# Batch 0's stored rows split by group, its gather and its constants in a new order on the DMA queue

## The chip, the cores and the metric

One core of a Trainium2 chip runs the kernel. The metric is the device time of one execution in microseconds (us), the median of several. Its engines each have a queue that is worked in order: TensorE (PE: matmuls, with the weight loads PEld beside them), VectorE (DVE), ScalarE (ACT), GpSimd (POOL) and SyncE (SP), which computes nothing here and issues every DMA.

## The reference

Eight batches of 3136 rows by 256 columns go through two stages. The first is a spectral layer: a real Fourier transform along the rows, a complex 256x256 mix with bias, a soft threshold, and the transform back. The second is a feed-forward layer with a three-tap convolution in its gate.

```python
X = np.fft.rfft(x, axis=1)
Yr = Xr @ w_r - Xi @ w_i + b_r
Yi = Xr @ w_i + Xi @ w_r + b_i
Y  = sign(Y) * max(|Y| - 0.01, 0)           # real and imaginary part alike
y  = np.fft.irfft(Yr + 1j * Yi, n=3136, axis=1)
h  = max(y @ w_in, 0)
out = (h * sigmoid(conv3(h, conv_w))) @ w_out
```

## The kernel before

The transform of 3136 = 56 x 56 points is taken in two steps by matmuls with tables. All work of the spectral layer is cut in units of four: four of 28 row pairs (JC) in stage 1, four of 28 frequency units (UG) in stage 2, mix and stage 3. So each batch has NG = 7 pieces of either kind, and there are 56 items (batch, group).

- **Stage 1** (`stage1`, and `stage1_head` for batch 0): one piece of x, a tile `xr` of 112 partitions by 4 x 256, is multiplied with the table `f1` in two matmuls; the two results are copied to an SBUF tile (`a1`, in the head `ha0` to `ha6`) and stored in DRAM as `sc1[b]` (112 rows, 28, 256). A piece fills all 112 rows, but only four of the 28 columns.
- **Stage 2** (`load_a2`, `stage2`): group g of a batch needs 16 of the 112 rows of `sc1[b]`, namely rows 16g to 16g + 15, with all 28 columns, so parts of all seven pieces. `load_a2` gathers them in a tile `a2` in one DMA. 16 matmuls with the table `t2` (one slice per group, `load_t2(g)`) follow; ACT and DVE split the result in a high and a low part (`fh`, `fl`, with `d` for the difference of the two components).
- **Mix** (`mix`): 36 matmuls with the mix weights `wmix_hi` and `wmix_lo`; then DVE adds `bias` (`p1`) and makes the sums `v`, ACT and DVE the threshold, ACT and POOL the split for stage 3.
- **Stage 3** (`stage3`): 12 matmuls with the table `i1_hi`, `i1_lo`, one copy, and a store to `sc2[b]`. It runs three items behind stage 2. The table comes in seven pieces (`load_inv1`), each loaded to a staging tile with the tag `raw` (two buffers, which the raw mix weights `wm_raw` use too) and split by an ACT cast and a DVE subtraction.

The main loop runs over the items: load `a2` for item it + 2, stage 2 of it, in the first seven turns a piece of the inverse table and the next slice of `t2`, mix of it - 1, stage 3 of it - 3, and up to a few pieces of stage 1 of later batches (`p1` counts them). From item 3 on, some background work converts the feed-forward weights. The feed-forward layer follows the loop.

Ahead of the loop stands the start, which the change is about: `load_f1`; the seven x pieces of batch 0 (the first in two halves); then, all queued behind the last x load, `load_t2(0)`, `load_mix` (the loads of both mix weights, and their conversion: `wmix_hi` by ACT casts at L140, `wmix_lo` at L141 and `wm` at L157 by DVE), `load_bias` (four loads), and `stage1_head`, in which ACT evicts the first and DVE the second matmul of each piece and SP stores the piece whole (L267). Behind the last of these stores are queued two pieces of stage 1 of batch 1 and `load_a2` of items 0 and 1; behind the second of these, everything else.

The order within each engine's queue is made by a planner, once for the whole program, from the order in which the code is traced, the dependencies, and its own estimate of times. `tc.issue_after(ins)` adds an edge by hand: what is traced in its block goes behind `ins` in the queue of `ins`'s engine. A DMA that SP issues has one of eight completion counters; the counters are used in turn, so the n-th DMA is issued only when the one eight before it has landed. A DMA that reads what another wrote waits in SP's queue until that one has landed.

Of the kernel before, what the change touches and what calls it, by code (L numbers as in the profile page):

```python
# [24 lines left out]
UG = 4  # L25
NG = U // UG
JC = 4
# [68 lines left out]
def spectral_ffn_kernel(ctx: ExitStack, tc: tile.TileContext, x, w_r, w_i, b_r, b_i,  # L96
                        w_in, conv_w, w_out, fwd1, fwd2, inv1, inv2, out):
    nc = tc.nc
    K1, K2 = 2 * R, 2 * SP

    dram = ctx.enter_context(tc.tile_pool(name="dram", bufs=1, space=DRAM))
    sc1 = [dram.tile([K1, H, D], F32, name=f"sc1_{b}") for b in range(B)]
# [15 lines left out]
    with ExitStack() as ab:  # L118
# [20 lines left out]
        def split(dst_hi, dst_lo, src):  # L139
            nc.scalar.copy(dst_hi, src)  # L140
            nc.vector.tensor_tensor(dst_lo, src, dst_hi.bitcast(F32), op=ALU.subtract)  # L141
# [4 lines left out]
        def load_t2(g):  # L146
            nc.sync.dma_start(t2[:, g * UG:(g + 1) * UG, :], fwd2v[:, g * UG:(g + 1) * UG, :])

        def load_mix():

            raw = [stg.tile([P, NT, D], F32, name=f"wm_raw{k}", tag="raw", bufs=2) for k in range(2)]
            for k in range(2):
                nc.sync.dma_start(raw[k], (w_r, w_i)[k].rearrange("(t p) e -> p t e", p=P))
            split(wmix_hi[:, :, 0, :], wmix_lo[:, :, 0, :], raw[1])
            for k, op in ((1, ALU.subtract), (2, ALU.add)):
                w = stg.tile([P, NT, D], F32, name="wm", tag="wm")
                nc.vector.tensor_tensor(w, raw[0], raw[1], op=op)  # L157
                split(wmix_hi[:, :, k, :], wmix_lo[:, :, k, :], w)

        def load_bias():  # L160
            for c in range(2):
                for k in range(UG // 2):
                    nc.sync.dma_start(bias[:, c, k, :], (b_r, b_i)[c].partition_broadcast(P))
# [77 lines left out]
        def stage1(b, jc):  # L241

            xr, _ = load_x(s1p, b, jc, bufs=XRB)
            a1 = s1p.tile([K1, JC, D], F32, name="a1", bufs=2)
            for j in range(0, JC, 2):
                ps = ps1.tile([K1, 2, D], F32, name="ps_s1")
                nc.tensor.matmul(ps, f1, xr[:, j:j + 2, :], start=True, stop=True)  # L247
                nc.scalar.copy(a1[:, j:j + 2, :], ps)
            return nc.sync.dma_start(sc1[b][:, jc * JC:(jc + 1) * JC, :], a1)

        def stage1_head(xs, b=0):

            with tc.tile_pool(name="ha", bufs=1, reuse_waits="tile") as ha:
                for jc, xr in enumerate(xs):
                    a1 = ha.tile([K1, JC, D], F32, name=f"ha{jc}")
                    for j in range(0, JC, 2):
                        k = (jc * 2 + j // 2) % 4
                        if k < 3:
                            ps = psm.tile([K1, 2, D], F32, name="ps_s1h", tag=f"ps_mx{k}")
                        else:  # L260
                            ps = ps1.tile([K1, 2, D], F32, name="ps_s1")
                        nc.tensor.matmul(ps, f1, xr[:, j:j + 2, :], start=True, stop=True)
                        if j:
                            nc.vector.tensor_copy(a1[:, j:j + 2, :], ps)
                        else:
                            nc.scalar.copy(a1[:, j:j + 2, :], ps)
                    st = nc.sync.dma_start(sc1[b][:, jc * JC:(jc + 1) * JC, :], a1)  # L267
            return st

        def load_a2(b, g):  # L270
            a2 = a2p.tile([K1, UG, D], F32, name="a2")
            ld = nc.sync.dma_start(a2, sc1[b].rearrange("(u q) j d -> (q j) u d", q=4)[:, g * UG:(g + 1) * UG, :])
            return a2, ld
# [65 lines left out]
        nc.vector.memset(warm, 0.0)  # L339
        nc.scalar.activation(warm, warm, AF.Sigmoid)  # L340

        AHEAD = NG + 3
        items = [(b, g) for b in range(B) for g in range(NG)]
        n_it = len(items)
        WP0, LAST = 3, n_it - 6
        a2s = {}
        p1 = NG
        load_f1()
        with tc.tile_pool(name="hx", bufs=1, reuse_waits="tile") as hx:
            xh = []  # L350
            for p in range(NG):
                xr, ld = load_x(hx, 0, p, parts=2 if p == 0 else 1, tag=f"hx{p}")
                xh.append(xr)
            with tc.issue_after(ld.ins):
                load_t2(0)
                load_mix()
                load_bias()
                st = stage1_head(xh)
        with tc.issue_after(st.ins):
            for _ in range(2):  # L360
                stage1(*items[p1])
                p1 += 1
            for i in range(2):
                a2s[i], ld = load_a2(*items[i])
        ab.enter_context(tc.issue_after(ld.ins))
        wkf, wk, cab, io = [ab.enter_context(tc.tile_pool(name=nm, bufs=n, reuse_waits="tile"))
                            for nm, n in (("wkf", 2), ("wk", 2), ("cab", 1), ("io", 2))]
        i1_hi = cab.tile([K2, U, K1], F32R, name="i1_hi")
# [124 lines left out]
    for st in range(n_st + LAG):  # L493
        if st < n_st:
# [8 lines left out]
            if todo and f in (1, 4, 7):  # L503
                b, jg = todo.pop(0)
# [28 lines left out]
```

## Time and profile before

| | us |
|---|---|
| median of 3 runs | 1789.02 (1785.93 to 1789.36) |
| the profiled execution | 1792.41 |
| its span, first to last instruction | 1790.6 |
| TensorE busy in it | 1750.6 |
| VectorE busy in it | 1539.0 |
| ScalarE busy in it | 1225.7 |

The rows further down come from the one profiled execution; their times count from the first instruction of its span. In a row of the timeline stand the start, the duration, engine, line and operation, the tile written and those read, and in brackets the idle time before it and what ended that. An fp32 matmul leaves two records, so a piece of stage 1 has four. In the table of stretches "(x38)" is the number of records in the stretch, PEclk the granted share of TensorE's full clock (2.4 GHz; the lower level is 1.2), and the DMA share is that of 16 DMA engines.

### The profile page before, as it was taken

What the parts mean: (1) busy time and instruction counts of PE and PEld (TensorE: products, weight loads), DVE (VectorE), ACT (ScalarE), POOL (GpSimd) and SP (SyncE); (2) the same over time, 40 slices, a digit from 0 to 9 for tenths busy, and PEclk for the clock granted to TensorE, in tenths of its full rate; (3) what the DMA queues carried; (4) which work ended last, traced back from release to release, by engine and by line L of the source; (5) the groups of instructions that cost most, each with busy time, mean ns of one, the idle gap of its engine ahead of it and who ended that gap; (6) DMA issues with size and microseconds to landing.
All of it is one profiled execution on the core that took longest, in us unless ns stands there. A gap on an engine that the chain in (4) does not pass through costs nothing.

```text
span 1790.6 us, 29395 instructions
## 1 busy us (share of the span) xinstructions
PE 1750.6 (98%) x12096; PEld 1640.0 (92%) x12096; DVE 1539.0 (86%) x1840; ACT 1225.7 (68%) x1581; POOL 133.5 (7%) x60
## 2 busy tenths in 40 slices
PE   5989999999998999999999999999999999999998
PEld 2878889889988999999999999999999999999998
DVE  2989999999997888888888888888888888888887
ACT  2657766666665677777777677777767767777766
POOL 0112222222222000000000000000000000000000
PEclk8999999999999999999999999999999999999999
DMA  9766676676535111111011011111101111100001
GB/s 267 234 218 210 186 231 213 189 236 203 159 99 152 40 52 32 32 52 52 32 53 52 21 33 51 53 50 51 50 27 42 52 42 42 42 22 21 21 22 42
DMA packets 107382, 164.63 MB, mean 92 GB/s; under 512 B 8816, under 2 KB 86000, under 8 KB 107248
## 3 DMA queue, kind: packets, MB, share of 16 engines
q1 hardware_dynamic: 107248, 162.74, 29.8%
q8 instruction: 96, 1.57, 0.4%
q14 instruction: 38, 0.31, 0.1%
HBM read 85.65 MB, written 77.07 MB: 91 GB/s over the span
## 4 chain that ended last, share of the span: by engine, by line
PE 88%; DVE 6%; DMA 2%; issue 1%; ACT 1%; SPq 0%; ACTq 0%; DVEq 0%
PE acc L468 31%; PE ps_h L440 31%; PE ps_mx L306 10%; PE ps_s L421 5%; PE ps_s L282 4%; PE ps_s L247 4%; PE ps_s L333 3%; DVE v L315 2%; DMA i_raw<-in_inv_dram 1%; DVE fl L290 1%; DVE fl L288 1%; DVE p L311 1%; DVE v L321 1%; DMA sc<-ha 0%; DVE d L287 0%
## 5 line engine op out<-in xcount | busy, mean ns | idle before, releaser
L468 PE MATMUL acc<-wout,gh 128*128 128x256 f32 x3136 | 577.2, 283 | 0.0
L449 DVE SCALAR_TENSOR_TENSOR c<-h,cst_s,c 128x896 f32<-128x896 f32 x448 | 512.7, 1146 | 53.2 <-ACT c L447 52.2
L440 PE MATMUL ps_h<-yh,win 128*128 128x450 f32 x1792 | 552.0, 368 | 1.4 <-ACT yh L427 1.2
L468 PEld LDWEIGHTS acc<-wout,gh 128*128 128x128 f32 x3136 | 501.0, 191 | 6.8
L468 PE MATMUL acc<-wout,gl 128*128 128x256 f32 x1568 | 441.9, 283 | 0.0
L442 ACT ACTIVATE h<-ps_h 128x900 f32<-128x900 f32 x224 | 207.5, 926 | 266.9 <-PE ps_h L440 266.7
L440 PEld LDWEIGHTS ps_h<-yh,win 128*128 128x128 f32 x1792 | 340.1, 190 | 27.1 <-ACT yh L427 1.4
L440 PE MATMUL ps_h<-yl,win 128*128 128x450 f32 x896 | 329.7, 368 | 0.7 <-DVE yl L428 0.7
L468 PEld LDWEIGHTS acc<-wout,gl 128*128 128x128 f32 x1568 | 298.7, 191 | 0.2
L455 DVE TENSOR_TENSOR gl<-c,gh 128x896 fp32r<-128x896 f32 x224 | 242.8, 1088 | 56.4 <-ACT gh L454 52.5
L451 DVE TENSOR_TENSOR c<-h,c 128x896 f32<-128x896 f32 x224 | 243.2, 1086 | 48.9 <-ACT c L450 48.6
L454 ACT CAST gh<-c 128x896 fp32r<-128x896 f32 x224 | 209.8, 943 | 49.3 <-DVE c L451 49.3
L450 ACT ACTIVATE c<-c 128x896 f32<-128x896 f32 x224 | 213.3, 952 | 26.0 <-DVE c L449 23.0
L306 PE MATMUL ps_mx<-wmix_lo,fh 128*128 128x256 f32 x672 | 204.1, 304 | 0.0
L306 PE MATMUL ps_mx<-wmix_hi,fh 128*128 128x256 f32 x672 | 200.3, 298 | 1.0 <-DVE cw_e L188 0.7
L306 PE MATMUL ps_mx<-wmix_hi,fl 128*128 128x256 f32 x672 | 191.8, 287 | 6.4 <-DVE fl L290 6.2
L440 PEld LDWEIGHTS ps_h<-yl,win 128*128 128x128 f32 x896 | 169.9, 190 | 11.6 <-DVE yl L428 1.0
L447 ACT ACTIVATE c<-h,cst_s 128x896 f32<-128x896 f32 x168 | 175.5, 1044 | 2.5
L323 POOL TENSOR_TENSOR sl<-v,sh 128x1024 fp32r<-128x1024 f32 x56 | 133.3, 2380 | 437.2 <-PE ps_s L333 277.2
L315 DVE TENSOR_TENSOR v<-ps_mx,p 64x512 f32<-64x512 f32 x224 | 153.9, 687 | 3.3
L306 PEld LDWEIGHTS ps_mx<-wmix_hi,fl 128*128 128x128 f32 x672 | 128.0, 191 | 18.3 <-issue 9.7
L306 PEld LDWEIGHTS ps_mx<-wmix_lo,fh 128*128 128x128 f32 x672 | 128.8, 192 | 12.3 <-issue 12.3
(86 smaller groups left out, 2037.6 us busy)
## 6 DMA issues: line engine op xcount, KB each, us to landing
a<-sc SPq DMA_DIRECT2D x56, 448.0 KB, 4.8
sc<-z SPq DMA_DIRECT2D x56, 448.0 KB, 3.2
z<-sc SPq DMA_DIRECT2D x56, 448.0 KB, 3.7
xr<-in_x_dram SPq DMA_DIRECT2D x55, 448.0 KB, 4.9
out_dram<-o SPq DMA_DIRECT2D x27, 896.0 KB, 4.2
sc<-a SPq DMA_DIRECT2D x49, 448.0 KB, 5.1
sc<-ha SPq DMA_DIRECT2D x7, 448.0 KB, 5.8
win_bits<-in_moe_w_in_dram SPq DMA_DIRECT2D x4, 512.0 KB, 7.4
```

The lines of the kernel that those rows point to most:

```text
L306: nc.tensor.matmul(ps[c][:, k, :], lt, rh, start=(n == 0), stop=(n == len(mm) - 1))
L315: nc.vector.tensor_tensor(v[dst, :, k, :], ps[c][src], p1[src, c], op=ALU.add)
L323: SL_ENG.tensor_tensor(sl, v, sh.bitcast(F32), op=ALU.subtract)
L440: nc.tensor.matmul(ps[:, a, 0:CH + 2], lt, rh, start=(n == 0), stop=(n == len(mm) - 1))
L442: nc.scalar.activation(h, ps[:, :, 0:CH + 2], AF.Relu)
L447: nc.scalar.mul(c, h[:, :, 0:CH], cw[:, 0, f:f + 1])
L449: nc.vector.scalar_tensor_tensor(c, h[:, :, k:k + CH], cw[:, k, f:f + 1], c, op0=ALU.mult, op1=ALU.add)
L450: nc.scalar.activation(c, c, AF.Sigmoid)
L451: nc.vector.tensor_tensor(c, h[:, :, 1:CH + 1], c, op=ALU.mult)
L454: nc.scalar.copy(gh, c)
L455: nc.vector.tensor_tensor(gl, c, gh.bitcast(F32), op=ALU.subtract)
L468: nc.tensor.matmul(acc[m // 2][:, m % 2, :], lt[:, sl], rh[:, f, :], start=(f == 0 and n == 0 and m % 2 == 0), stop=(f == NF - 1 and n == ...
```

## The change

- The seven stores of batch 0 become fourteen: of each piece, the 16 rows that group 0 needs (`rows` 0 to 15) are stored apart from the other 96.
- These stores stand in an order written out by hand, each queued behind the one before: the 16 rows of pieces 0 to 4, the other rows of piece 0, the 16 rows of piece 5, the other rows of piece 1, the 16 rows of piece 6, then the gather `load_a2` of item 0, then the other rows of pieces 2 to 6.
- Behind the last store stands the gather of item 1, behind it the four bias loads, the two pieces of stage 1 of batch 1 (with their x loads), and all the rest.
- The two raw mix weights are loaded ahead of the first slice of `t2`, and converted (`make_mix`) behind the last two evictions of the head on ACT and DVE.

No byte more or less is moved, and no matmul, copy or addition is added or removed.

```diff
--- before.py
+++ after.py
@@ -147,10 +147,13 @@
             nc.sync.dma_start(t2[:, g * UG:(g + 1) * UG, :], fwd2v[:, g * UG:(g + 1) * UG, :])
 
         def load_mix():
-
             raw = [stg.tile([P, NT, D], F32, name=f"wm_raw{k}", tag="raw", bufs=2) for k in range(2)]
             for k in range(2):
                 nc.sync.dma_start(raw[k], (w_r, w_i)[k].rearrange("(t p) e -> p t e", p=P))
+            return raw
+
+        def make_mix(raw):
+
             split(wmix_hi[:, :, 0, :], wmix_lo[:, :, 0, :], raw[1])
             for k, op in ((1, ALU.subtract), (2, ALU.add)):
                 w = stg.tile([P, NT, D], F32, name="wm", tag="wm")
@@ -250,9 +253,13 @@
 
         def stage1_head(xs, b=0):
 
+
+            KG = 4 * UG
             with tc.tile_pool(name="ha", bufs=1, reuse_waits="tile") as ha:
+                a1s, evs = [], []
                 for jc, xr in enumerate(xs):
                     a1 = ha.tile([K1, JC, D], F32, name=f"ha{jc}")
+                    a1s.append(a1)
                     for j in range(0, JC, 2):
                         k = (jc * 2 + j // 2) % 4
                         if k < 3:
@@ -261,11 +268,24 @@
                             ps = ps1.tile([K1, 2, D], F32, name="ps_s1")
                         nc.tensor.matmul(ps, f1, xr[:, j:j + 2, :], start=True, stop=True)
                         if j:
-                            nc.vector.tensor_copy(a1[:, j:j + 2, :], ps)
+                            ev = nc.vector.tensor_copy(a1[:, j:j + 2, :], ps)
                         else:
-                            nc.scalar.copy(a1[:, j:j + 2, :], ps)
-                    st = nc.sync.dma_start(sc1[b][:, jc * JC:(jc + 1) * JC, :], a1)
-            return st
+                            ev = nc.scalar.copy(a1[:, j:j + 2, :], ps)
+                        evs.append(ev)
+                order = [(jc, 0) for jc in range(NG - 2)] + [(0, 1), (NG - 2, 0), (1, 1), (NG - 1, 0), None]
+                order += [(jc, 1) for jc in range(2, NG)]
+                last = None
+                for o in order:
+                    with ExitStack() as pin:
+                        if last is not None:
+                            pin.enter_context(tc.issue_after(last.ins))
+                        if o is None:
+                            a2s[0], last = load_a2(*items[0])
+                        else:
+                            jc, rest = o
+                            rows = slice(KG, K1) if rest else slice(0, KG)
+                            last = nc.sync.dma_start(sc1[b][rows, jc * JC:(jc + 1) * JC, :], a1s[jc][rows])
+            return last, evs[-2:]
 
         def load_a2(b, g):
             a2 = a2p.tile([K1, UG, D], F32, name="a2")
@@ -339,11 +359,11 @@
         nc.vector.memset(warm, 0.0)
         nc.scalar.activation(warm, warm, AF.Sigmoid)
 
+        a2s = {}
         AHEAD = NG + 3
         items = [(b, g) for b in range(B) for g in range(NG)]
         n_it = len(items)
         WP0, LAST = 3, n_it - 6
-        a2s = {}
         p1 = NG
         load_f1()
         with tc.tile_pool(name="hx", bufs=1, reuse_waits="tile") as hx:
@@ -352,17 +372,18 @@
                 xr, ld = load_x(hx, 0, p, parts=2 if p == 0 else 1, tag=f"hx{p}")
                 xh.append(xr)
             with tc.issue_after(ld.ins):
+                wm_raw = load_mix()
                 load_t2(0)
-                load_mix()
-                load_bias()
-                st = stage1_head(xh)
+                st, evs = stage1_head(xh)
+        with tc.issue_after(evs[0].ins), tc.issue_after(evs[1].ins):
+            make_mix(wm_raw)
         with tc.issue_after(st.ins):
-            for _ in range(2):
-                stage1(*items[p1])
-                p1 += 1
-            for i in range(2):
-                a2s[i], ld = load_a2(*items[i])
+            a2s[1], ld = load_a2(*items[1])
         ab.enter_context(tc.issue_after(ld.ins))
+        load_bias()
+        for _ in range(2):
+            stage1(*items[p1])
+            p1 += 1
         wkf, wk, cab, io = [ab.enter_context(tc.tile_pool(name=nm, bufs=n, reuse_waits="tile"))
                             for nm, n in (("wkf", 2), ("wk", 2), ("cab", 1), ("io", 2))]
         i1_hi = cab.tile([K2, U, K1], F32R, name="i1_hi")
```

## Rows read from the trace of the kernel before

**Rows 1.** The page's part 1: busy time, share of the span and instructions of each engine.

```profile
PE 1750.6 (98%) x12096; PEld 1640.0 (92%) x12096; DVE 1539.0 (86%) x1840; ACT 1225.7 (68%) x1581; POOL 133.5 (7%) x60
```

**Rows 2.** Busy time of each engine in stretches, with records, clock, DMA share and rate.

```profile
core 0: us, PE busy (x) PEld busy (x) DVE busy (x) ACT busy (x) POOL busy (x), PEclk, DMA share, GB/s
20.00:24.00 4.00, 1.98 (x4) 0.54 (x4) 3.88 (x7) 2.78 (x6) 0.00 (x0) 1.00 0.98 380
20.00:36.70 16.70, 4.00 (x6) 0.99 (x6) 4.92 (x8) 3.56 (x7) 0.00 (x0) 0.67 0.96 312
36.70:45.00 8.30, 8.26 (x38) 6.94 (x39) 3.89 (x7) 3.85 (x9) 0.00 (x0) 0.63 1.07 281
45.00:70.00 25.00, 24.76 (x180) 21.62 (x178) 22.41 (x37) 14.46 (x27) 2.39 (x1) 1.00 1.01 300
70.00:95.00 25.00, 23.70 (x170) 20.80 (x170) 23.18 (x33) 17.74 (x30) 7.20 (x3) 1.00 0.48 154
95.00:120.00 25.00, 20.46 (x125) 16.48 (x126) 22.72 (x29) 14.47 (x22) 7.47 (x3) 0.93 0.72 211
120.00:200.00 80.00, 80.00 (x583) 70.59 (x583) 75.89 (x121) 54.35 (x89) 17.61 (x8) 1.00 0.69 218
```

**Rows 3.** Timeline of SP's queue, 17 to 35 us: when DMAs are issued.

```profile
18.16 7.46 SPq L267 DMA_DIRECT2D sc<-ha  x7
25.67 3.20 SPq L238 DMA_DIRECT2D xr<-in_x_dram  x2
31.54 1.40 SPq L272 DMA_DIRECT2D a<-sc  x3
...
33.52 0.55 SPq L147 DMA_DIRECT2D t<-in_fwd_dram  x1
```

**Rows 4.** Timeline of TensorE's matmuls, in three stretches up to 118 us.

```profile
12.32 2.74 PE L262 MATMUL ps_s1h<-xr,f 112*112 112x512 f32 x6
14.90 1.02 PE L262 MATMUL ps_s<-xr,f 112*112 112x512 f32 x2
...
20.92 1.98 PE L262 MATMUL ps_s1h<-xr,f 112*112 112x512 f32 x4 [1.57 <-ACT ha L266]
...
36.74 3.78 PE L282 MATMUL ps_s<-t,a 112*128 112x128 f32 x16 [1.50 <-DMA a<-sc]
...
50.10 0.28 PE L306 MATMUL ps_mx<-wmix_hi,fl 128*128 128x256 f32 x1
50.22 1.95 PE L282 MATMUL ps_s<-t,a 112*128 112x128 f32 x16
...
113.05 0.38 PE L333 MATMUL ps_s<-sh,i_hi 128*112 128x256 f32 x1 [1.92 <-ACT z L335]
```

**Rows 5.** Timeline of ACT and DVE, from 17 to 62 us.

```profile
19.76 0.62 ACT L140 CAST wmix_hi<-wm_raw 128x512 fp32r<-128x512 f32 x1 [4.08 <-DMA wm_raw<-in_w_i_dram]
...
24.35 0.68 DVE L264 COPY ha<-ps_s1h 112x512 f32<-112x512 f32 x1
...
50.78 2.80 DVE L315 TENSOR_TENSOR v<-ps_mx,p 64x512 f32<-64x512 f32 x4
```

**Rows 6.** DMA issues: short windows from 31.5, 33.5, 67.5 us, then the page's part 6.

```profile
a<-sc SPq DMA_DIRECT2D x3, 448.0 KB, 6.5
...
t<-in_fwd_dram SPq DMA_DIRECT2D x1, 224.0 KB, 8.2
...
xr<-in_x_dram SPq DMA_DIRECT2D x1, 448.0 KB, 3.6
...
sc<-z SPq DMA_DIRECT2D x56, 448.0 KB, 3.2
```

**Rows 7.** Stretch 36.7 to 45 us, matmuls of the mix (L306) alone.

```profile
36.70:45.00 8.30, 2.77 (x10) 1.87 (x10) 0.63 1.07 281
```

**Rows 8.** The chain that ended last, up to 140 us: start, duration, what.

```profile
45.89 8.55 DMA i_raw<-in_inv_dram
...
65.57 4.46 DMA i_raw<-in_inv_dram
```

**Rows 9.** Waits of ACT, 36 to 120 us: total, times, longest.

```profile
ACT i_hi L140 <- DMA i_raw<-in_inv_dram: 8.7, 7, 2.4
```

## The prediction, before the changed kernel ran

> **What bounds the kernel now.** I read the busy shares first. TensorE is busy in 98% of the span [rows 1], so a change can only pay by removing time in which TensorE has nothing to do, or runs at the low clock. The table of stretches says where that is: from 120 us on TensorE takes 583 matmul records in 80 us, 7.29 per us, without a gap [rows 2]. Against that pace the start is thin. Between 20 and 36.7 us there are 6 records, from 36.7 to 45 us 38 at a granted clock of 0.63 (the low level, 1.2 GHz, for most of it), from 45 to 70 us 180 of a possible 182, from 70 to 95 us 170, and from 95 to 120 us only 125. The two last shortfalls are 12 and 57 records, 1.7 and 7.8 us.
>
> Next I looked at what the first hole is made of. DMA runs at a share of 0.96 between 20 and 36.7 us and at 1.0 until 70 us, so the start is a queue of bytes: the order in SyncE's queue decides what TensorE can do. SyncE issues the seven head stores from 18.16, two x loads of batch 1 from 25.67, and the first gathers of stored rows (a2) at 31.54, when the last store has landed; the first stage-2 matmul starts at 36.74, released by that gather [rows 3, 4].
>
> In the head itself the ACT row at 19.76 waited 4.08 us for a mix weight, and head evictions stand behind it in the queue; TensorE waits for one of them until 20.92, and the last DVE eviction ends at 24.35 + 0.68 = 25.03 [rows 4, 5].
>
> **The change, part by part.**
>
> *Mix weights last.* Head matmuls run 0.43 us a record ((14.90 - 12.32) / 6), two records a matmul [rows 4]. Twelve of the fourteen matmuls have been issued by about 19.2; without the stall the last two follow at once and end near 20.9, and the last eviction near 21.7 instead of 25.0: 3.3 us. The conversions (three ACT casts, five DVE operations of about 0.68 us, as the last DVE row of the same width, 3.4 us in all [rows 5]) then run from 21.7 to about 26, under the wait for a2; the mix of group 0 needs them no earlier than 32. Cost 0, and 3.4 us if that cover were gone.
>
> *Split stores.* Seven stores become fourteen: 64 KB (16 rows) and 384 KB (96 rows). Seven more issues of SyncE at some 0.4 us stand in time in which it waits for evictions. At the rate of the store stretch (380 GB/s [rows 2]) 64 KB are 0.17 us. No DMA of 16 rows stands in the trace, so its price is bounded: 0.17 us by bytes, or as long as a whole store by the same rate, 1.2 us. I take the lower, since 4 KB runs per row stay as they are; the upper is a rival below. The Trainium skill speaks against the lower one (SBUF — State Buffer, "Door 1: The DMA port swizzle"): the rate depends on how many SBUF ports the rows reach, and rows 0 to 15 reach 4 of 16, some 109 GB/s. By that the estimate for one small store is 0.6 us, and the seven cost 3 us more than in my sum; no row here shows it.
>
> *First gather.* The last small store can go at 21.9, behind two 384 KB stores that are moving by then. A lightly loaded 448 KB transfer lands 3.2 to 3.6 us after its issue [rows 6], 1.2 of it bytes, so a small one takes some 2: landed 23.9. The gather goes at 24.1 and lands after 3.6 (light) to 5.2 (31.54 to 36.7 [rows 3, 4]): 27.7 to 29.3. I take 27.9, 8.8 us before 36.7.
>
> *Second gather.* Behind the first gather go five stores of 384 KB, 1.97 MB, 5.2 us at 380 GB/s; they have landed at about 33. SyncE stands in the wait for that, and everything else is queued behind: bias, the two x loads, the third gather, the first inverse table, t2 of group 1. Nothing then covers the end of the stores, as the x loads did before (25.67, issued six us ahead of the gather). The second gather lands at 33.1 + 3.7 = 36.8, against about 31.9 (the second of the three issues at 31.54) + 6.5 = 38.4 [rows 3, 6].
>
> *What comes behind.* Ahead of and including t2 of group 1 go 0.52 (bias) + 0.92 (x) + 0.46 + 0.23 + 0.23 = 2.36 MB, at 281 GB/s [rows 2] 8.4 us: t2 of group 1 lands at 45.2, against 33.52 + 8.2 = 41.7 [rows 3, 6]. That is 3.5 us late. The bytes ahead of it are the same in both kernels, so this is the price of two drains of the DMA queue, one before each gather. It holds for all that follows until the queue is empty (about 70 us). Bias lands near 38.7, before the first mix has its sums; hidden. The x loads of batch 1 land near 40.3 and 42; now they go ahead of the first gather.
>
> **The sum.** TensorE's ledger at 45 us, at full-clock prices (16 stage-2 records 1.8 us, a mix record 0.12, an x unit 4 x 0.43 [rows 4]). Before, since the head: 24 stage-2 records, 10 mix records and three x matmuls (38 records in the stretch 36.7 to 45 [rows 2], ten of them mix [rows 7], and one x matmul ahead of it): 2.7 + 1.2 + 2.6 = 6.5 us. After: stage 2 and the mix of group 0 (36 records) and two x units: 1.8 + 4.3 + 3.4 = 9.5 us, also when half of it runs at the low clock, since 17 us are there. Lead 3.0 us. From 45.2 the work in hand (groups 1 and 2, 12.2 us; an x unit 1.7; two stage-3 groups 2.8) lasts until about 62, when the next gather has landed; I take 1 us off for evictions it must wait for. Lead 2.
>
> DVE leads too: before it adds bias and sums group 0 only from 50.78 (four operations, 2.80 us [rows 5]), after some 8 us earlier, in time in which it was idle (3.89 us busy of 8.3 [rows 2]). Those 2.8 us count in the stretches from 70 to 120 us, where DVE is busy for 22.7 to 23.2 of 25 us and TensorE falls short. Together -4.8 us.
>
> Against it stands the inverse table. Its staging tile has two buffers, so every load waits for the split two groups before; the trace has 8.55 us (45.89) and 4.46 us (65.57) of it in the chain that ended last, and ACT sat 8.7 us in seven waits for it between 36 and 120 us [rows 8, 9]. ACT runs in order, so evictions stand behind. This chain begins with table 0, which is 3.5 us late; as the queue empties towards 70 us I let it recover one: +2.5.
>
> Sum: -4.8 + 2.5 = -2.3 us, taken as -2. The profiled execution is 1792.4 us (span 1790.6 and 1.8 around it), so 1790.4; the median of the runs is 3.4 below that execution: 1787.0. 0.2% is 3.6 us, what a measurement can tell here (the three runs spread by 3.4).
>
> **Rivals.**
>
> *A, the forecast*: early group 0, half of it given back at the inverse tables. 1785.4 to 1790. Chance 0.38.
>
> *B, the lead carries*: ACT's casts of the tables come behind the evictions in the new order, so the late tables hold nobody. For it: stage 3 needs table 0 only three groups later. Then -4.8, and up to the whole 8.8 us if the waits at 95 to 120 us vanish as well (TensorE waits until 113.05 for an ACT copy, 1.92 us [rows 4]): 1780.2 to 1784.2. Chance 0.30.
>
> *C, slower*: TensorE's queue is in order, and t2 of group 1 gates it. Now stage-2 matmuls of group 1 stand amid the mix of group 0. If they do so again, mix 0 waits for 45.2 and the lead of 3.0 is never made, while everything is 3.5 us late: 1792.5. It decides from the point where t2 of group 1 lands over 3.0 us late. Against it: the order is made anew with gather 0 well ahead. Chance 0.16.
>
> *D, dear small stores*: 1.2 us each, 7 x 1.03 = 7.2 us more on the queue; gather 0 near 33, t2 of group 1 past 50. The lead is gone: +4 to +7, 1793 to 1796. Against it: the rows are as long as before and only fewer. Chance 0.08. The rule of the Trainium skill cited above (SBUF — State Buffer, the same section) would make it 3 us by its estimate, and the end +1.
>
> *E, nothing moves*: TensorE's order puts an x matmul of batch 1 ahead of group 0, as now one precedes 36.74; it waits for 40.3, and gain and loss cancel: 1789. Chance 0.08.
>
> **Numbers.** Likeliest is A: 1787.0. Faster by over 0.2%: B and a tenth of A, 0.34. Slower: D and most of C, 0.22. The rest, 0.44, is within 0.2%. Leaving out a third of B and most of D gives 1781.5 to 1793.0; A alone is 1785.4 to 1790.
>
> **What would show it.** Last head eviction near 21.7; first stage-2 matmul near 28 (33 speaks for D); t2 of group 1 landing near 45; two dips of the DMA share near 24 and 34; some 20 more matmul records between the head and 45 us than now (16 + 36 + 8, against 38 + 2); the shortfall at 95 to 120 us smaller than 57 records (B: under 25). The prediction falls if the order of the later groups, which is planned anew for the whole kernel, opens or closes waits far from the start, at the change from one phase to the next above all.

## The result: slower, outside the range

The median went from 1790.64 us (13 runs, 1785.93 to 1792.48) to 1799.67 us (13 runs, 1790.35 to 1802.73). The ratio is 1.0043, with a 95% interval of 1.0028 to 1.0058: slower by 5 to 10 us, where 1787.0 was forecast with a range up to 1793.0. The profiled execution took 1800.78 us, its span is 1799.0, 8.4 us above the span before. The times of the changed kernel are spread: eight of the 13 are at 1798.0 to 1802.7, five at 1790.4 to 1796.4, and both profiles of it below (1800.78 and 1800.95) are of the upper part. In the ratios further down, executions more than 1.5% above the fastest of their kernel are left out, eight at 1822 to 1825 us of three versions; one at 1822.67 lies just inside and lifts the ratio of the bias early.

The busy shares answer to [rows 1]: the same work, spread over a longer span.

```profile
PE 1755.7 (98%) x12096; PEld 1645.3 (91%) x12096; DVE 1539.3 (86%) x1840; ACT 1225.2 (68%) x1581; POOL 133.3 (7%) x60
```

The table of stretches of the changed kernel, to be laid beside [rows 2]; three more stretches are added.

```profile
20.00:24.00 4.00, 1.69 (x4) 0.35 (x2) 2.88 (x5) 1.72 (x3) 0.00 (x0) 0.99 0.77 236
20.00:36.70 16.70, 10.04 (x51) 8.56 (x50) 7.39 (x12) 4.67 (x9) 0.00 (x0) 0.69 0.69 224
36.70:45.00 8.30, 0.82 (x7) 0.61 (x6) 0.93 (x2) 0.00 (x0) 0.00 (x0) 0.76 0.86 154
45.00:70.00 25.00, 19.96 (x109) 15.73 (x110) 13.79 (x23) 11.49 (x22) 2.39 (x1) 0.74 1.06 283
70.00:95.00 25.00, 24.59 (x172) 20.93 (x172) 24.63 (x36) 17.85 (x31) 4.76 (x2) 1.00 0.70 223
95.00:120.00 25.00, 22.18 (x143) 18.74 (x142) 23.46 (x33) 13.82 (x20) 6.42 (x3) 0.93 0.62 182
120.00:200.00 80.00, 79.85 (x578) 70.03 (x577) 75.75 (x118) 56.27 (x94) 20.07 (x9) 1.00 0.73 227
...
37.81:44.67 6.86, 0.00 (x0) 0.00 (x0) 0.69 (x1) 0.00 (x0) 0.00 (x0) 0.73 0.87 136
...
200.00:540.00 340.00, 337.11 (x2527) 304.74 (x2526) 317.16 (x521) 230.23 (x367) 87.58 (x37) 1.00 0.63 190
...
540.00:600.00 60.00, 51.71 (x365) 48.92 (x364) 41.88 (x73) 31.32 (x37) 11.92 (x5) 0.91 0.42 123
```

Group 0 does come early: 51 records between 20 and 36.7 us, where [rows 2] have 6. Then there is nothing to do: 7 records up to 45 us (38 before) and 109 up to 70 (180 before). In 37.81 to 44.67 us TensorE starts no matmul at all, and the queue moves 136 GB/s at a DMA share of 0.87: not idle, but slow.

The timeline of SyncE's queue, TensorE, VectorE and ScalarE in the changed kernel, beside [rows 3], [rows 4] and [rows 5]. L287 is a head store, L292 a gather, L166 the bias, L241 a load of x, L147 a slice of `t2`.

```profile
17.33 5.45 SPq L287 DMA_DIRECT2D sc<-ha  x6
24.63 0.32 SPq L292 DMA_DIRECT2D a<-sc  x1
25.00 5.22 SPq L287 DMA_DIRECT2D sc<-ha  x5
34.23 0.32 SPq L292 DMA_DIRECT2D a<-sc  x1
34.60 0.96 SPq L166 DMA_DIRECT2D bias<-in_b_r_dram  x2
35.60 0.91 SPq L166 DMA_DIRECT2D bias<-in_b_i_dram  x2
36.55 0.90 SPq L241 DMA_DIRECT2D xr<-in_x_dram  x2
...
41.69 0.86 SPq L147 DMA_DIRECT2D t<-in_fwd_dram  x1
...
28.35 3.75 PE L302 MATMUL ps_s<-t,a 112*128 112x128 f32 x16 [6.66 <-DMA a<-sc]
...
46.73 2.05 PE L250 MATMUL ps_s<-xr,f 112*112 112x512 f32 x2 [9.21 <-DMA xr<-in_x_dram]
52.09 3.75 PE L302 MATMUL ps_s<-t,a 112*128 112x128 f32 x16 [3.31 <-DMA t<-in_fwd_dram]
...
21.73 0.69 DVE L271 COPY ha<-ps_s1h 112x512 f32<-112x512 f32 x1 [1.02 <-PE ps_s1h L269]
...
40.47 0.69 DVE L331 TENSOR_TENSOR p<-ps_mx,bias 128x512 f32<-128x512 f32 x1 [5.64 <-DMA bias<-in_b_r_dram]
44.77 0.69 DVE L331 TENSOR_TENSOR p<-ps_mx,bias 128x512 f32<-128x512 f32 x1 [3.61 <-DMA bias<-in_b_i_dram]
...
51.86 0.63 DVE L141 TENSOR_TENSOR i_lo<-i_raw,i_hi 128x448 fp32r<-128x448 f32 x1 [6.40 <-ACT i_hi L140]
52.40 2.81 DVE L335 TENSOR_TENSOR v<-ps_mx,p 64x512 f32<-64x512 f32 x4
...
51.26 0.56 ACT L140 CAST i_hi<-i_raw 128x448 fp32r<-128x448 f32 x1 [17.16 <-DMA t<-in_fwd_dram]
```

The two waits of TensorE, 9.21 us for an x piece and 3.31 us for `t2` of group 1, are the hole. Between them stand two records of x, one matmul. How late the loads are is read from the DMA issues (last column: us from issue to landing), here for the last bias load, issued at 36.07, and for `t2` of group 1:

```profile
bias<-in_b_i_dram SPq DMA_DIRECT2D x1, 128.0 KB, 8.6
...
t<-in_fwd_dram SPq DMA_DIRECT2D x1, 224.0 KB, 10.3
```

The second gather landed at 37.81, the four bias loads at 38.52, 40.35, 42.63 and 44.67, the two x loads at 46.69 and 48.47, and `t2` of group 1 at 51.95. So the four bias loads, 0.52 MB, landed over 6.86 us, and everything behind them came late. The queue was not theirs alone in that time: of the 0.93 MB that it moved, 0.57 MB were x, in packets of 4 KB, all of them from 42 us on. From 40 to 42 us it moved packets of 1 KB only, 0.11 MB in 2 us, 57 GB/s.

VectorE's add of the bias (L331) waits for each half. ScalarE's cast of the first inverse table stands first in its queue until 51.26; VectorE's part of that table stands ahead of the sums of group 0 and waits 6.40 us for the cast, so the sums (L335) start at 52.40, where [rows 5] have 50.78.

**Where the 8.4 us lie.** I keep TensorE's ledger as in the prediction: the time, minus the full-clock price of all matmul records begun by then (0.43 us a stage-1 record, 0.112 in stage 2, 0.12 in the mix, 0.118 in stage 3, and 0.112, 0.204 and 0.12 for the three kinds of matmul behind the loop). What is lost so far, in us:

| lost by (us) | 36.7 | 45 | 60 | 120 | 540 | 600 |
|---|---|---|---|---|---|---|
| before | 23.8 | 26.5 | 26.9 | 36.5 | 40.6 | 53.6 |
| changed kernel | 19.1 | 26.8 | 36.0 | 42.1 | 46.3 | 61.6 |

The changed kernel leads by 4.7 us at 36.7, has lost the lead at 45, is 9.1 behind at 60 and gets 3.5 back by 120 us, where before loses too. 5.6 us of the difference are made by then, none between 120 and 540, 2.3 at the change of phases (540 to 600 us, where the granted clock was 0.91 against 0.94 before), and 0.5 elsewhere.

### The profile page after: what moved, and what is told of

It is laid out like the page before. It is cut to its first block, busy times and chain, and to the rows that moved or that the text cites. A ratio compares the mean times of both kernels' runs of the same rounds, so it can differ in the third digit from the quotient of the medians.

```text
span 1799.0 us, 29400 instructions
## 1 busy us (share of the span) xinstructions
PE 1755.7 (98%) x12096; PEld 1645.3 (91%) x12096; DVE 1539.3 (86%) x1840; ACT 1225.2 (68%) x1581; POOL 133.3 (7%) x60
## 4 chain that ended last, share of the span: by engine, by line
PE 89%; DVE 6%; issue 2%; DMA 2%; ACT 1%; SPq 0%; ACTq 0%; DVEq 0%
PE acc L489 31%; PE ps_h L461 31%; PE ps_mx L326 10%; PE ps_s L442 5%; PE ps_s L302 4%; PE ps_s L250 4%; PE ps_s L353 3%; DVE v L335 1%; DVE fl L310 1%; DVE fl L308 1%; DVE v L341 1%; DMA t<-in_fwd_dram 1%; PE ps_s1h L269 1%; DVE p L331 0%; DVE d L307 0%
## 5 line engine op out<-in xcount | busy, mean ns | idle before, releaser
L461 PEld LDWEIGHTS ps_h<-yh,win 128*128 128x128 f32 x1792 | 340.4, 190 | 26.8 <-ACT yh L448 1.4
L472 DVE TENSOR_TENSOR c<-h,c 128x896 f32<-128x896 f32 x224 | 243.3, 1087 | 48.8 <-ACT c L471 48.5
L335 DVE TENSOR_TENSOR v<-ps_mx,p 64x512 f32<-64x512 f32 x224 | 153.7, 686 | 3.4
L302 PEld LDWEIGHTS ps_s<-t,a 112*128 112x128 f32 x896 | 111.8, 197 | 33.1 <-issue 23.7
```

The lines of the kernel that those rows point to most:

```text
L302: nc.tensor.matmul(ps[:, k], a2[:, k, t * P:(t + 1) * P], t2[:, g * UG + k, :], start=(k == 0), stop=(k == UG - 1), skip_group_check=True)
L335: nc.vector.tensor_tensor(v[dst, :, k, :], ps[c][src], p1[src, c], op=ALU.add)
L461: nc.tensor.matmul(ps[:, a, 0:CH + 2], lt, rh, start=(n == 0), stop=(n == len(mm) - 1))
L472: nc.vector.tensor_tensor(c, h[:, :, 1:CH + 1], c, op=ALU.mult)
```

## Experiments

The theory after the first profile: each of the four bias loads reads one row of 1 KB 128 times (`partition_broadcast`), and such loads are slow when little else is in the queue; in this place they delay x and `t2` of group 1. Rivals: the time comes from the order of bytes alone, from the two empty stretches of the DMA queue, from the small stores, or from the order of the engines, which is planned anew. All medians stand in one table, with the landing of `t2` of group 1 and TensorE's loss by 60 and by 120 us in the profiled run.

| run | t2 of group 1 lands | lost by 60 | by 120 | median (runs) | ratio to before, 95% |
|---|---|---|---|---|---|
| before | 41.70 | 26.9 | 36.5 | 1790.64 (13) | 1 |
| changed kernel | 51.95 | 36.0 | 42.1 | 1799.67 (13) | 1.0043 (1.0028 to 1.0058) |
| the same again | 51.42 | 34.5 | 42.7 | 1800.54 (4) | 1.0064 (1.0046 to 1.0081) |
| 128 rows | 47.77 | 31.3 | 31.6 | 1790.73 (12) | 1.0008 (0.9993 to 1.0024) |
| 128 rows again | 45.68 | 29.1 | 35.3 | 1791.1 (10) | 1.0014 (0.9996 to 1.0031) |
| before, 128 rows | 39.78 | 26.3 | 32.0 | 1789.57 (10) | 1.0001 (0.9985 to 1.0017) |
| two loads | 47.79 | 32.2 | 34.3 | 1792.18 (10) | 1.0004 (0.9991 to 1.0018) |
| bias twice | 55.97 | 37.9 | 44.3 | 1800.74 (4) | 1.0050 (1.0032 to 1.0069) |
| bias behind x | 48.68 | 32.3 | 34.8 | 1795.7 (4) | 1.0044 (1.0026 to 1.0061) |
| before, bias late | 43.74 | 27.4 | 34.1 | 1794.02 (6) | 1.0027 (1.0012 to 1.0041) |
| before, mix last | 42.05 | 26.9 | 37.9 | 1789.43 (12) | 1.0000 (0.9989 to 1.0012) |
| bias early | 45.73 | 31.8 | 35.9 | 1823.03 (6) | 1.0105 (1.0046 to 1.0165) |
| bias in the middle | 46.41 | 31.2 | 38.2 | 1795.86 (10) | 1.0027 (1.0013 to 1.0042) |
| the same, 128 rows | 45.27 | 29.9 | 36.6 | 1796.2 (10) | 1.0031 (1.0018 to 1.0044) |
| bias early, x as cover | 45.91 | 29.6 | 34.3 | 1788.64 (11) | 0.9993 (0.9984 to 1.0003) |
| and t2 ahead of x | 37.44 | 29.3 | 38.3 | 1788.88 (11) | 1.0004 (0.9994 to 1.0014) |

(The kernel before took 1790.37, 1788.88, 1788.56, 1789.41 and 1789.54 us in the five later comparisons, and each ratio is to the one of its own.) A ledger is that of one execution: before and its twin with 128 rows, with the same order on TensorE, VectorE and ScalarE, have 36.5 and 32.0 at 120 us, in executions of 1792.41 and 1787.44 us, while their medians lie within 1 us. So a single ledger at 120 us tells a version from another no better than to some 4 us.

### The rows of the bias loads

```diff
-                    nc.sync.dma_start(bias[:, c, k, :], (b_r, b_i)[c].partition_broadcast(P))
+                    nc.sync.dma_start(bias[:, c, k, :], x[2 * c + k][0:P, :])
```

In the changed kernel (order on TensorE, VectorE and ScalarE unchanged):

> The changed kernel, with each bias tile loaded from 128 different rows of x (same size, same pieces of 1 KB, same place in the queue) instead of 128 times the same row; it leaves out the true bias. The queues of all engines are the same as in the changed kernel. Same row: the four loads land 0.4 to 0.5 us apart, t2 of group 1 near 47, and the time falls 4 to 6 us under the changed kernel. Rival (any small pieces behind a drain are slow, or loads beside late stores are): they land about 2 us apart as in the changed kernel, t2 of group 1 near 52, the time as in the changed kernel.

The four loads landed at 36.90, 38.40, 38.96 and 39.70 instead of 38.52 to 44.67. Of this run, the stretch of the bias loads alone and four stretches as above:

```profile
36.70:39.70 3.00, 0.00 (x0) 0.00 (x0) 0.69 (x1) 0.00 (x0) 0.00 (x0) 0.80 0.95 250
...
36.70:45.00 8.30, 2.05 (x2) 0.45 (x2) 1.38 (x2) 0.00 (x0) 0.00 (x0) 0.61 1.00 250
45.00:70.00 25.00, 21.90 (x142) 19.03 (x143) 18.82 (x32) 16.43 (x30) 2.39 (x1) 0.86 1.06 307
70.00:95.00 25.00, 25.00 (x179) 21.52 (x178) 24.65 (x39) 19.20 (x33) 7.48 (x3) 1.00 0.62 204
95.00:120.00 25.00, 24.79 (x180) 21.57 (x179) 21.94 (x34) 16.32 (x26) 7.13 (x3) 1.00 0.84 261
```

And TensorE's waits between 36.7 and 60 us (us in total, times, longest):

```profile
PE ps_s L250 <- DMA xr<-in_x_dram: 6.0, 1, 6.0
PE ps_s L302 <- DMA t<-in_fwd_dram: 3.3, 1, 3.3
```

In the stretch of the bias loads the queue now moves 250 GB/s where it moved 136, the wait for x is 6.0 instead of 9.2 us, and the median is 9 us lower, more than the 4 to 6 expected. That is nearly the whole loss of the change. Two controls and a repeat:

> The changed kernel once more, with a second profile. Same row: the four bias loads again take 6 to 7 us and t2 of group 1 lands at 50 us or later; the time is 1796 to 1803 in most executions. Rival (the first profile showed a chance event): the bias loads land within 3 us, t2 of group 1 before 48, and the slow median has another cause.

> The kernel before with each bias load fetching 128 different rows of x (the sums then lack the true bias, and other values go through the threshold). Control for the run with 128 rows in the new order. Theory of the one row: here the bias loads hide behind a deep queue in either form, t2 of group 1 lands at 41 to 41.7, and the time stays at 1789, within 2 us. Rival, the other values and not the rows made that run faster: some 9 us less, near 1780.

> The changed kernel with 128 different rows in each bias load once more (the sums lack the true bias), beside the early placement on the same chip. Theory of the one row: 1788 to 1793 again, t2 of group 1 landing near 47.8, TensorE's ledger at 120 us near 32. Rival, the run of 1790.7 was a lucky set of the clock at the change of phases: 1795 or more.

The changed kernel came out at 1800 again, the one with 128 rows at 1791 again, and in the order of before the rows make no difference (1789.57): neither chance nor the values, but the rows that the loads read, and these only in the new place. The order of the bytes, the small stores, the two empty stretches of the DMA queue and the order on the engines are the same in the runs with 128 rows, and these lie 0.4 and 1.6 us above before, with both intervals around 1; so none of those rivals makes the 9 us. One is left: the 128 rows come from x, the one row from `b_r` or `b_i`. No run read one row of x 128 times, so the repeated row and the place of these two vectors in memory are not told apart.

The hole is not all of the 9 us. Between the profiles of the changed kernel and of the one with 128 rows, first and second, TensorE's loss differs by 4.7 and 5.4 us at 60 us, by 10.5 and 7.4 at 120, and by 2.7 and 2.5 more at the change of phases.

### How much of it: two loads, eight loads

Two loads, the second half of each tile copied on the core:

```diff
-                for k in range(UG // 2):
-                    nc.sync.dma_start(bias[:, c, k, :], (b_r, b_i)[c].partition_broadcast(P))
+                nc.sync.dma_start(bias[:, c, 0, :], (b_r, b_i)[c].partition_broadcast(P))
+                nc.gpsimd.tensor_copy(bias[:, c, 1, :], bias[:, c, 0, :])
```

> The changed kernel with two bias loads instead of four (one of each vector, 128 KB), and the second half of each tile copied from the first on GpSimd. Theory of the one row: 3.4 us are gone from the queue, bias has landed near 41.2, t2 of group 1 lands near 48.6; about half of the way from the changed kernel to the one with 128 distinct rows, near 1795. Rival, plain bytes: 0.26 MB less are 0.9 us, t2 near 51, near 1799. Rival, the start doesn't set the time: within 2 us of 1800.

Eight loads:

```diff
         load_bias()
+        load_bias()
         for _ in range(2):
```

> The changed kernel with the four bias loads issued twice over, in the same place (0.52 MB more). Theory of the one row: each 128 KB load of one row takes 1.6 to 1.9 us more, so the eight take 13.5 us behind the second gather, t2 of group 1 lands near 58.5 (51.95 with four), TensorE stands idle 6.5 us longer, and the time is 5 to 7 us above that of the changed kernel, near 1806. Rival, plain bytes: 0.52 MB more at 281 GB/s are 1.9 us, t2 near 53.9, near 1802. Rival, the start doesn't set the time (the later phases do): t2 late, the time within 2 us of 1800.

With two loads the queue is 4 us earlier (47.79, where 48.6 was expected), but 1792 is nearer to the free rows (1791) than half way. With eight, one x load went ahead of the second four; `t2` of group 1 landed at 55.97 (58.5 expected), and the time did not move: 1800.7, where the theory had 1806 and the rival "the start doesn't set the time" 1800. The stretches of the run with eight, from 45 to 120 us and at the change of phases:

```profile
45.00:70.00 25.00, 18.03 (x84) 12.80 (x85) 13.73 (x20) 9.64 (x18) 2.37 (x1) 0.66 0.97 263
70.00:95.00 25.00, 25.00 (x188) 22.52 (x187) 24.67 (x37) 18.22 (x32) 4.77 (x2) 1.00 0.75 233
...
540.00:600.00 60.00, 51.53 (x388) 49.14 (x387) 44.41 (x78) 34.00 (x39) 12.28 (x6) 0.97 0.42 125
```

Of 4.0 us more in the landing 2.2 are left by 120 us (188 records from 70 to 95 us against 172), and 3.0 came back at the change of phases, at a clock of 0.97 instead of 0.91. So the loss does not grow in proportion. With the bias directly behind the second gather it is 0 to 4 us at a landing of 45.7 to 47.8, 9 to 12 at 52, and no more at 56. The order on the engines was planned anew for two and for eight loads, and only the runs with 128 rows keep that of the changed kernel, so the shape of this curve stays open.

### The bias loads in other places

Behind the two x loads:

```diff
-        load_bias()
         for _ in range(2):
             stage1(*items[p1])
             p1 += 1
+        load_bias()
```

> The changed kernel with the four bias loads behind the two x loads of batch 1 instead of ahead of them; nothing else. In step (the row is read slowly only when all 16 DMA engines come to it at once, fresh from a drained queue): behind 0.92 MB of x the engines are apart, the four loads cost some 2 us of the queue, t2 of group 1 lands near 47, and the time is 3 to 6 us under the changed kernel. Always (a load of one row 128 times takes 1.7 us wherever it stands): t2 of group 1 lands near 52 as in the changed kernel, the bias later still, and the time is the same or worse.

They are late there too: landed at 39.70, 40.75, 43.32 and 44.98, 5.5 us behind the last x load (39.45), `t2` of group 1 at 48.68, and the time between the two levels above. The stretch from that x load on:

```profile
39.45:45.00 5.55, 1.67 (x8) 1.37 (x7) 0.00 (x0) 0.00 (x0) 0.00 (x0) 0.50 0.53 138
```

The rate is near that of the changed kernel (136), at a share of 0.53 instead of 0.87. So neither expectation fits as it stands: the loads are slow behind x as well, and the time is still 4 to 5 us under the changed kernel. And in the kernel before, moved from ahead of the head stores to behind the second gather:

```diff
                 load_mix()
-                load_bias()
                 st = stage1_head(xh)
...
         ab.enter_context(tc.issue_after(ld.ins))
+        load_bias()
```

> The kernel before with one part of the change alone: the four bias loads behind the gathers of groups 0 and 1 instead of ahead of the head stores. Always: the loads take 6 to 7 us there, t2 of group 1 lands near 46 instead of 41.7, and the time grows by 2 to 5 us. In step: behind a full queue they cost 2 us as they did ahead, the gather of group 0 lands some 1 us earlier, and the time is within 2 us of the kernel before.

They took 3.6 us for the four (36.79 to 40.42), between the 2 and the 6 to 7 expected; `t2` of group 1 landed 2.0 us later, and the kernel is 5 us slower by the medians: moving the bias makes the kernel before lose as well. How much of the 5 us is the late `t2` and how much the order, which the planner made anew here too, this run does not tell.

### Undoing the place

```diff
                 load_t2(0)
+                load_bias()
                 st, evs = stage1_head(xh)
...
         ab.enter_context(tc.issue_after(ld.ins))
-        load_bias()
```

> The changed kernel with the four bias loads back ahead of the head stores, behind the first slice of t2; all else of the change stays. Theory (same row): behind the drained queue, every one of the 128 descriptors of a bias load reads the same 1 KB row at the same moment, and the four loads take 6.9 us (37.8 to 44.7) instead of about 2; ahead of the stores the DMA engines are out of step and the reads hide among others. Then t2 of group 1 lands near 46 instead of 52, TensorE stands some 5 us better at 60 us, and the time is 4 to 7 us under the changed kernel, about 1793 to 1796. Rival (drains): the loss is the two drains and the order of later DMAs, not the bias; the bytes moved forward by 0.5 MB give t2 of group 1 about 2 us, and the time stays within 2 us of the changed kernel.

The loads landed as expected and the start was 6 us better by 120 us, but five of the six runs took 1823 to 1825 and one 1795.8, so that this run does not price the place: its median cannot be laid beside the others. In the profiled execution (1823.04) the loss lies far behind the start, in 200 to 540 us:

```profile
200.00:540.00 340.00, 320.12 (x2319) 281.73 (x2317) 331.77 (x476) 212.75 (x341) 82.32 (x35) 1.00 0.60 180
```

These are 2319 records of TensorE, where the changed kernel has 2527, at the same granted clock. What puts an execution there is not shown. The place was then undone in a second way, with the loads free behind the last x load, and that once more from 128 rows. The expectation took this for another order on the engines; in the traces the order on TensorE, VectorE, ScalarE and GpSimd is the same as in the run above, and only the fourth bias load stands elsewhere in SyncE's queue, behind the first small store.

```diff
+            xld = ld
             with tc.issue_after(ld.ins):
...
+        with tc.issue_after(xld.ins):
+            load_bias()
         ab.enter_context(tc.issue_after(ld.ins))
-        load_bias()
```

> The changed kernel with the bias loads free to go anywhere behind the last x load of batch 0: they are traced at the same place as in the changed kernel but stand in SyncE's queue behind t2 of group 0, the fourth behind the first small store. A second way to undo only the place of the bias, with another order on the engines than that of the bias loads moved by hand, which came out at 1823. Theory of the one row: bias has landed near 20, t2 of group 1 near 46, TensorE's ledger at 120 us is 4 to 10 us better than in the changed kernel (42), and if the order keeps the 9.2 us an item, the time is 1787 to 1793. Rival, the early place itself makes the items dear (10 us each from 200 to 540 us, by DVE's order): near 1823 again.

> The bias loads early (behind t2 of group 0, as in the run before this one, with the same order on TensorE, VectorE and ScalarE), and each fetching 128 different rows of x (so the sums lack the true bias). Theory of the order: the 4 to 5 us that are left in the early placement come with the order of the engines behind 60 us; the time stays at 1794 to 1797, and TensorE loses some 6 us or more between 60 and 120 us. Rival, the one row costs wherever it stands in the new order (stores and first gather behind it are late): first gather lands 28 instead of 29.1, and the time falls to 1788 to 1791.

Eight of ten runs at 1793 to 1798 with either rows, the other two at 1822 to 1825; 1787 to 1793 had been expected of the first. So an early bias saves about 4 us of the 9 here, and 5 us are left in this version, whatever the rows. They come with its order on the engines or in the DMA queue, which no run parts; that the first gather lands later (28.54 with 128 rows, against 27.22 and 26.87 with the late bias) is not enough, since the version with x as cover, below, has it at 29.11 and loses nothing. In the profiled run with 128 rows there are 144 records in 95 to 120 us, where the late bias with 128 rows had 180 and 146 in its two profiles, and the clock is 0.91 at the change of phases (0.97 in both of those). Its stretches:

```profile
95.00:120.00 25.00, 22.18 (x144) 19.00 (x143) 21.92 (x29) 14.64 (x21) 5.72 (x3) 0.93 0.77 223
...
540.00:600.00 60.00, 51.70 (x349) 48.34 (x347) 42.80 (x70) 33.63 (x37) 9.55 (x5) 0.91 0.41 123
```

### Covering the second drain, and the parts alone

Bias early, and the two x loads between the last store and the second gather:

```diff
         with tc.issue_after(st.ins):
+            for _ in range(2):
+                stage1(*items[p1])
+                p1 += 1
             a2s[1], ld = load_a2(*items[1])
...
-        for _ in range(2):
-            stage1(*items[p1])
-            p1 += 1
```

> As e1_bias_early, and the two x loads of batch 1 stand between the last store and the second gather, as in the kernel before, so that they cover the wait for the last store. Drains: the second dip of DMA goes, t2 of group 1 lands near 44 (2 us ahead of e1), the second gather near 38.5, and the time is some 2 us under e1. Same row alone: the drain is hidden anyway, as TensorE has group 0 to do; the time is within 1 us of e1. If both hold it ends near the kernel before, 1788 to 1792.

The same with `t2` of group 1 ahead of these x loads (and no longer in the loop):

```diff
         with tc.issue_after(st.ins):
+            load_t2(1)
             for _ in range(2):
```

> The version that the runs so far point to: the changed kernel with the bias early (as e3), and t2 of group 1 as well as the two x loads between the last store and the second gather. t2 of group 1 lands near 38 instead of 45.9 in e3, the second gather near 43, and it gates stage 2 of group 1 alone: TensorE's ledger at 60 us some 2 us better than e3, the time 1785 to 1788. Rival: DMA order among these loads no longer matters once the second gather is the last to land; then as e3, 1788 to 1789.

These came out at 1788.6 and 1788.9, level with before and no better; 1785 to 1788 had been expected of the second. `t2` of group 1 8 us earlier (37.44 against 45.91) gained nothing. Against the early bias without this cover (1795.9) they are 7 us faster. That is not the price of the second empty stretch: the order on the engines is another in each of them, and in the first the second gather landed at 42.27 instead of 38.5 and `t2` at 45.91 instead of 44. And the kernel before with only the mix weights converted last:

```diff
-                load_mix()
+                wm_raw = load_mix()
...
+        with tc.issue_after(evs[0].ins), tc.issue_after(evs[1].ins):
+            make_mix(wm_raw)
```

> The kernel before with one part of the change alone: the mix weights are converted behind the head's last evictions. Expected by the prediction's step: the last head eviction near 22 instead of 25.0, the last store near 29 instead of 31.5, the first stage-2 matmul 1 to 3 us earlier, and 0 to 3 us less time. Rival: the queue of bytes is full all the same (share 0.96), so the gather lands within 0.5 us of 36.7 and the time is the same.

The last head eviction ended at 22.3, as expected, and the time did not change: the last store landed at 30.32 instead of 31.47, and the first gather at 36.30 instead of 36.70.

## Why the prediction was wrong

The step that failed is "What comes behind": 2.36 MB at 281 GB/s, `t2` of group 1 at 45.2, and "Bias lands near 38.7, before the first mix has its sums; hidden". The mis-sized term is the bias. Priced by its bytes, 0.52 MB were 1.9 us; by their landings the four loads took 6.9, and `t2` came at 51.95 instead of 45.2. The 6.75 us between these are 1.0 (the second gather landed at 37.8, not 36.8), 5.0 (bias) and 0.7 (the 1.84 MB behind landed over 7.3 us, not 6.5). The runs with 128 rows show that this term cost the 9 us.

A second term was wrong on its own, and it is why the gain is missing even in those runs. The sum counted two x units (8 records, 3.4 us) by 45 us, ahead of group 1. In TensorE's queue only one x matmul (2 records, 0.9 us) stands there; the rest of x comes behind the stage-2 matmuls of group 1, and so behind `t2`. With 128 rows x had landed at 42.46, yet the row of 36.7 to 45 us above has 2 records, and TensorE then waited 3.3 us for `t2`. Without the other 2.6 us the lead of 3.0 is 0.4 at most, about what the 128 rows have at 45 us (26.0 lost, 26.5 before).

Rows of before that I did not read could have warned of the bias. These three stand around the last moments of its bias loads, when x had landed (18.07) and the second mix weight was about to (19.74):

```profile
14.00:18.00 4.00, 4.00 (x11) 1.69 (x10) 1.38 (x2) 0.59 (x1) 0.00 (x0) 1.00 1.07 256
...
19.00:20.00 1.00, 0.35 (x1) 0.00 (x0) 0.16 (x1) 0.24 (x1) 0.00 (x0) 1.00 0.58 105
20.00:22.00 2.00, 1.08 (x3) 0.48 (x4) 2.00 (x4) 1.87 (x4) 0.00 (x0) 1.00 1.01 404
```

The queue moved 256 GB/s while x and the weights were moving with them, 105 GB/s when the bias loads were nearly alone, 404 GB/s with the stores. At 105 GB/s 0.52 MB are 5.0 us. A queue that runs empty shows a low rate as well, so this was a hint and no proof. I took the rate of a stretch of other transfers for a load of a kind that stood in the trace.

Point by point:

- **Mix weights last, first gather**: right. Last head eviction at 21.73 + 0.69 = 22.4 (21.7), first gather landed 28.2 (27.9), first stage-2 matmul 28.35 (28). The mix of group 0 was through at 37.5. Both dips were there: near 24 and 34 us.
- **The small stores' price**: the last one was issued at 22.48 and landed at 24.51, 2.0 us as taken, and 0.6 us late by its issue. The first that moved alone (issued at 17.33, 16 packets of 4 KB) was through in 0.7 us (18.14 to 18.84), at 222 to 554 ns a packet, where those of whole stores before had a median of 159: nearer to the estimate of 0.6 us by the Trainium skill (SBUF — State Buffer, "Door 1: The DMA port swizzle") than to 0.17. It did not reach the sum, since each waits for its eviction. Rival D fell.
- **The lead**: there at 36.7 us (4.7 us), and gone at 45, where 3.0 was forecast. The x units that were to fill the time landed at 46.7 and 48.5 instead of 40.3 and 42. Even where they came at 40.8 and 42.5 (128 rows, repeat), the ledger at 45 us was 26.0 against 26.5: the lead of 3.0 at 45 us was made in no run of the new order. No version came out clearly faster than before, so the -4.8 is not shown by any of them.
- **DVE's lead**: there was none. The sums of group 0 came at 52.40, 1.6 us later than before: VectorE had the bias added at 45.46 and then waited 6.40 us for the cast of the first inverse table, a wait that the prediction did not count.
- **The inverse table**: later than priced. ScalarE stood 17.16 us in front of table 0, where [rows 9] have 8.7 us in seven waits. It had little else to do in that time, but VectorE's sums hung on it. What this cost of the 2.5 us in the sum no run shows by itself.
- **Rivals**: C came nearest. Its sign is right, and the lead is gone since TensorE's queue is in order; but TensorE was held 9.21 us by x and then 3.31 by `t2` of group 1, the mix of group 0 was through at 37.5 and not held, and the size and the cause (the bias) are not those of C. The prediction had `t2` 3.5 us late and C decide beyond 3.0, and still gave it 0.16. The point from which it decides was wrong as well: with 128 rows and with two loads the time is 0 to 4 us above before at a landing of 47.8, 6.1 us late.
- **Far from the start**: 2.3 of the 8.4 us lie at the change of phases, as the prediction had named as a way to fall. In the order of the changed kernel these 60 us cost TensorE 15.3 and 15.2 us in its two profiles, and 12.6 and 12.7 with 128 rows, so there they went with the bias loads. Over all versions the cost is between 11 and 17 us, at a granted clock of 0.89 to 0.97, and what links it to the start is not shown.

Open: why the loss is so steep between 47.8 and 52 us, how the 5 us of the late bias in the kernel before divide, and what costs 5 us in the version with the early bias.

## What to carry to other kernels

Before a load is moved from a full DMA queue to an empty one, look at how it reads: here a broadcast of one row cost nothing among other transfers and some 9 us behind an empty queue, so price such a load from a stretch in which little else moves, and lay 128 different rows beside it as a control. When a rival's own condition is already met by your forecast of it (3.5 us late where 3.0 decide), its chance is not small. Look as well at what stands next in the queue of the engine that is to use the time: work that comes early is worth only what the next work in the queue can follow it with; here group 0 was 8 us earlier, one matmul stood behind it, and TensorE waited for x and the next table.

## What the runs showed of the hardware

- A load of 128 KB that reads one row of 1 KB for all 128 partitions took 1.8 to 2.3 us in the changed kernel (the second to the fourth, landed from 38.52 to 44.67, with x beside the last of them). Four such loads took 6.9 us there, 5.5 behind two x loads, 3.6 in the old order behind the gathers. In the changed kernel the 1 KB packets took up to 842 ns, with medians of 166 to 346 ns from 40 to 43 us, against 46 ns from 36 to 38, when the gather and the first of them moved. From 128 different rows four loads took 3.0 and 2.7 us (36.70 to 39.70 and 36.58 to 39.25). The Trainium skill (DMA: Bandwidth & Descriptors, "Latency and other measured facts") has copies at 207 to 103 GB/s when the rows lie 512 KiB to 8 MiB apart, at powers of two, and at the full rate again with 4 KiB of padding; it puts this down, as an inference, to streams that meet on one channel of the memory. No run here varies the distance, and none shows where the packets wait.
- A VectorE subtraction of two SBUF tiles (`fl<-d,fh`, 128 x 512) took 0.68 to 0.69 us in 34 of 37 cases in the changed kernel from 200 to 540 us. The other three took 1.3, 2.6 and 2.8 us, each while GpSimd worked on a subtraction of its own (`sl<-v,sh`, 2.4 us).
